# SwiGLU feed-forward on one core: full-array transposes at the start, a transposing load in two parts, and F tile 0 of the last token tiles in strips

## The chip, the cores and the metric

The kernel runs on one core of a Trainium2 chip. A core has a matrix engine (TensorE, "PE" in the profile, with its weight loads as "PEld"), VectorE ("DVE"), ScalarE ("ACT"), GpSimd ("POOL") and a queue engine that issues transfers (SyncE, "SP"). The metric is the device time of one execution in microseconds, as the median of several runs.

## The reference

```python
B, S, D, F = 1, 2048, 512, 1376       # x: (B, S, D); all inputs bfloat16

def reference(x, w_gate, w_up, w_down):
    g = silu(x @ w_gate)              # (S, F)
    u = x @ w_up                      # (S, F)
    return (g * u) @ w_down           # (S, D)
```

## The kernel before

The 2048 tokens are worked on in four chunks `c` of 512 (`SC`). D = 512 is four tiles of 128 (`KD`). F = 1376 is ten whole tiles of 128 (`NFF`) and a rest of 96. Gate and up products are computed with F on the partitions: for a chunk and an F tile there is a G group (gate) and a U group (up), each of four matmuls into one PSUM bank. ScalarE takes the silu of the G bank, VectorE multiplies it with the U bank and writes `hT_sb`. The rest of 96 is handled in X and Y groups, whose results stand in `hx_sb` and `hy_sb`. Groups take the eight PSUM banks in turn, and a bank is free when its reader eight groups earlier is done (`free`).

The order on each engine is written out by hand, and semaphores connect the engines: `s_P` counts finished groups of TensorE, `s_A` and `s_D` finished operations of ScalarE and VectorE, `s_X` finished transposes, `s_T` the turns told of below, and each load has one of its own.

The matmuls need x with D on the partitions (`xT_sb`). Tokens 0 to 255 come by two plain loads (`xn0` on SP, `xn1` on ACT) and are transposed on TensorE with an identity (L347). `RT` says in how many row pieces: the first 128 tokens go as two pieces of 64 rows, the second as one of 128. The transposes write PSUM, and for each 128 tokens VectorE (L292) and ScalarE (L281) copy two D tiles each into `xT_sb`. Ahead of that, TensorE multiplies constants (`warm`, L336): five matmuls of 512 columns and five of 128, and one of 128 (`N_COPY`) after the transposes. Tokens 256 to 511 come by one transposing load on SP (`x0b`, L93), which is queued behind the weight slabs of F tiles 0 to 3 and ahead of those of tiles 4 to 10. The three other chunks are transposing loads of 512 tokens each. All loads on SP but the first are issued in one stream without waits.

The first eight groups (F tiles 0 to 3, chunk 0) run in two passes: first over tokens 0 to 255, where the first group goes in two parts of 128 tokens, and then over tokens 256 to 511, which needs `x0b`. From then on every group takes 512 tokens at once.

The down product has tokens on the partitions of the output: 16 token tiles of 128, in four quads `q` of four tiles, one from each chunk. Its contraction has 43 pieces of 32 rows. In `strips` (L423), four matmuls of 32 rows run beside each other in four row groups of TensorE, each for another token tile of the quad and in another bank: this is a round. A call `strips(q, k, fks, ...)` is a phase: it makes one round for each F tile in `fks`, all with the row groups turned by `k`; the entry `NFF` is the rest of F. Ahead of the next phase of the same quad TensorE waits on `s_T` until the last round of the phase before is done (a turn). Quads 0 and 1 alternate phases. Quad 2 has phases of 10 or 11 rounds, and between two of them stands a phase of quad 3 with one round, the rest of F. What is left of quad 3 (F tiles 0 to 9) is then done with whole matmuls of 128 rows (L459), tile by tile; the last token tile is in two parts of 384 and 128 columns. Results are copied to `o_sb` by VectorE and ScalarE in turn, and SP stores them.

Of the kernel before, what the change touches and what calls it, by code (L numbers as in the profile page):

```python
# [8 lines left out]

N_WARM = 5  # L10
N_FILL = 5
N_COPY = 1


def bass_standalone__swiglu_ffn__prompt_kernel(nc, x, w_gate, w_up, w_down, out):
    _, S, D = x.shape
    F = w_gate.shape[1]
    P = 128
    KD = D // P
    NFF = F // P  # L20
    NFT = NFF + 1
    F_LAST = F - NFF * P
    SC = 512
    NSC = S // SC
    TPC = SC // P
    NST = S // P
    LASTA = 384
    HT = SC // 2
    NXN = HT // P
# [20 lines left out]
    with ExitStack() as es:  # L50
# [32 lines left out]
        def load_sem(name):  # L83
            loads[name] = sem(f"s_{name}")
            return loads[name]
# [6 lines left out]
        def load_x(eng, name, t0, t1):  # L92
            eng.dma_start_transpose(  # L93
                xT_sb[:, :, t0:t1], xf[t0:t1, :]
            ).then_inc(load_sem(name), 16)
# [10 lines left out]
        def load_gate(eng, a, b):  # L106
            load_w(eng, f"wg{a}", w_gate, 0, a * P, min(b * P, F))
# [4 lines left out]
        def load_xn(eng, i):  # L112
            eng.dma_start(xn_sb[:, i, :], xf[i * P:(i + 1) * P, :]).then_inc(load_sem(f"xn{i}"), 16)
# [5 lines left out]
        def loads_on_sync(sp):  # L119
            load_xn(sp, 0)  # L120
            load_gate(sp, *slabs[0])
            for a, b in slabs[1:3]:
                load_gate(sp, a, b)
                load_up(sp, a, b)
            load_x(sp, "x0b", HT, SC)
            for a, b in slabs[3:]:
                load_gate(sp, a, b)
                load_up(sp, a, b)
            load_w(sp, "wut", w_up, F - (F - 32), F - 32, F)
            for c in range(1, NSC):  # L130
                load_x(sp, f"x{c}", c * SC, (c + 1) * SC)
            sp.dma_start(
                wd_sb[:, 0:NFF, :], w_down[0:NFF * P, :].rearrange("(k p) d -> p k d", p=P)
            ).then_inc(load_sem("wd"), 16)
            load_sem("wdt")
            for y0 in (0, 64):
                sp.dma_start(wd_sb[y0:y0 + 64, T01, :], w_down[NFF * P:F - SR, :]).then_inc(loads["wdt"], 16)
            for x0 in range(0, P, SR):
                sp.dma_start(wd_sb[x0:x0 + SR, T2, :], w_down[F - SR:F, :]).then_inc(loads["wdt"], 16)
            sp.dma_start(wd_sb[0:F_LAST, TAIL, :], w_down[NFF * P:F, :]).then_inc(load_sem("wdl"), 16)  # L140
# [16 lines left out]
            g["readers"].append((eng, op["at"]))  # L157
            return op

        RT = [2, 1]  # L160
        T_BANK = [0, 2 * RT[0]]

        def tview(i, h):
            n, b0 = RT[i], T_BANK[i] + RT[i] * h
            return bank_all[:, b0:b0 + n, 0:P // n].bitcast(BF16).rearrange("p b (k t) -> p k b t", k=2)
# [47 lines left out]
        for i in range(NXN):  # L213
            for h, eng in enumerate("DA"):
                op = add_op(
                    eng, dict(readers=[]), kind="copy", ready=(s_X, 2 * sum(RT[:i]) + RT[i] * (h + 1)),
                    out=xT_sb[:, 2 * h:2 * h + 2, i * P:(i + 1) * P].rearrange("p k (b t) -> p k b t", b=RT[i]),
                    src=tview(i, h), stored=(None, 0),
# [13 lines left out]
        for at, t in enumerate(tiles):  # L232
            ob = at % NOS
            need = 16 * n_store[ob]
            halves = [(0, D)] if at < NST - 1 else [(0, LASTA), (LASTA, D)]
            for c0, c1 in halves:
                g = add_group("O", t=t, c0=c0, c1=c1)
                eng = "A" if at % 2 == 1 and c0 == 0 else "D"
                op = add_op(
                    eng, g, kind="copy", out=o_sb[ob][:, c0:c1], src=g["bank"][:, 0:c1 - c0],  # L240
# [54 lines left out]
        def on_tensor(pe):  # L295
            landed = set()

            def need(name, count=1):
                if name not in landed:
                    pe.wait_ge(loads[name], 16 * count)  # L300
                    landed.add(name)
# [13 lines left out]
            def gu_matmuls(g, n0, n1):  # L315
                c, ft = g["c"], g["ft"]
                if c > 0:
                    need(f"x{c}")
                if c == 0 and n1 > HT:
                    need("x0b")  # L320
                need(("wg" if g["kind"] == "G" else "wu") + str(slab_of[ft]))
                col = (0 if g["kind"] == "G" else UPH) + ft * P
                for dk in range(KD):
                    if c == 0 and dk % 2 == 0:
                        for i in range(n0 // P, min(n1 // P, NXN)):
                            after(*xt_ready[i, dk // 2])
                    ins = pe.matmul(  # L327
                        g["bank"][:, n0:n1], lhsT=w_sb[:, dk, col:col + P],
                        rhs=xT_sb[:, dk, c * SC + n0:c * SC + n1], start=(dk == 0), stop=(dk == KD - 1),
                    )  # L330
                if n1 == SC:
                    ins.then_inc(s_P, 1)

            def warm(n, width):
                for i in range(n):
                    pe.matmul(banks[NB - 1][:, 0:width], lhsT=ones_w, rhs=ones_m[:, 0:width], start=True, stop=True)  # L336
# [4 lines left out]
            for i in range(NXN):  # L341
                need(f"xn{i}")
                for dk in range(KD):
                    for b in range(RT[i]):
                        rt = P // RT[i]
                        r0 = rt * b
# [5 lines left out]
                        if dk % 2 == 1:  # L352
                            ins.then_inc(s_X, 1)

            warm(N_COPY, P)
            first = groups[0:NB]
            for n0, n1 in ((0, P), (P, HT)):
                gu_matmuls(first[0], n0, n1)
            for at in (1, 2, 3, 4, 6, 5, 7):
                gu_matmuls(first[at], 0, HT)  # L360
            for g in first:
                gu_matmuls(g, HT, SC)

            for g in groups[NB:NO]:
# [4 lines left out]
                elif kind == "X":  # L369
                    c = g["c"]  # L370
                    need(f"wg{slab_of[NFF]}")
                    need("wut")
                    for dk in range(KD):
# [3 lines left out]
                            start=(dk == 0), stop=(dk == KD - 1),  # L377
                        )
                    ins.then_inc(s_P, 1)
                elif kind == "Y":  # L380
                    need(f"wu{slab_of[NFF]}")
                    for dk in range(KD):
                        for c in (2 * g["pi"], 2 * g["pi"] + 1):
# [4 lines left out]
                                start=(dk == 0), stop=(dk == KD - 1),  # L388
# [8 lines left out]
                spare = (P + SR - 2 * Y_ROWS[c] - X_ROWS[c]) // SR  # L397
                return (spare + k) % TPC

            def strips(q, k, fks, start, stop):  # L400
                nonlocal n_turn
                quad = groups[NO + TPC * q:NO + TPC * (q + 1)]
                if start:
                    for g in quad:
                        free(g)
                else:
                    pe.wait_ge(s_T, turned[q])
                for fk in fks:
                    if fk == NFF:
                        need("wdt", 2 + TPC)  # L410
                    for c, g in zip(ORDER, quad):
                        t, c0, c1 = g["t"], g["c0"], g["c1"]
                        r0 = SR * strip_of(c, k)
                        tok = (t - c * TPC) * P
                        if fk < NFF:
                            h, w = hT_sb[r0:r0 + SR, fk, t * P:(t + 1) * P], fk
                        else:
                            after("D", t_ready[c])
                            if r0 == X_ROWS[c]:
                                h, w = hx_sb[r0:r0 + SR, c, tok:tok + P], T2  # L420
                            else:
                                h, w = hy_sb[r0:r0 + SR, c // 2, tok:tok + P], T01
                        ins = pe.matmul(  # L423
                            g["bank"][:, 0:c1 - c0], lhsT=h, rhs=wd_sb[r0:r0 + SR, w, c0:c1],
                            start=(start and fk == fks[0]), stop=(stop and fk == fks[-1]),
                            tile_position=(r0, 0), skip_group_check=True,
                        )
                        if stop and fk == fks[-1]:
                            ins.then_inc(s_P, 1)
                if not stop:  # L430
                    ins.then_inc(s_T, 1)
                    n_turn += 1
                    turned[q] = n_turn
# [4 lines left out]
            full, tailed = list(range(NFF)), list(range(NFT))  # L438
            for k in range(TPC):
                for q in (0, 1):  # L440
                    strips(q, k, full if k == 0 else tailed, k == 0, k == TPC - 1)
            for k in range(TPC):
                strips(2, k, full if k == 0 else tailed, k == 0, k == TPC - 1)
                if k < TPC - 1:
                    strips(3, k + 1, [NFF], k == 0, False)
            pe.wait_ge(s_T, turned[3])
            for g in groups[NO + TPC * (TPC - 1):]:
                t, c0, c1 = g["t"], g["c0"], g["c1"]
                last = g is groups[-1]
                if last:  # L450
                    free(g)
                    need("wdl")
                    pe.wait_ge(s_L, 1)
                for fk in (tailed if last else full):
                    if fk < NFF:
                        h, w = hT_sb[:, fk, t * P:(t + 1) * P], wd_sb[:, fk, c0:c1]
                    else:
                        h, w = hl_sb[0:F_LAST, :], wd_sb[0:F_LAST, TAIL, c0:c1]
                    ins = pe.matmul(  # L459
                        g["bank"][:, 0:c1 - c0], lhsT=h, rhs=w, start=(last and fk == 0),  # L460
                        stop=(fk == (NFF if last else NFF - 1)), skip_group_check=True,
                    )
                ins.then_inc(s_P, 1)
# [34 lines left out]
```

## Time and profile before

| what | value |
|---|---|
| median of 3 runs | 120.95 us (120.3 to 121.28) |
| the profiled execution | 120.11 us |
| its span in the profile | 118.8 us |
| TensorE busy | 115.5 us, 97% of the span, 982 matmuls |
| weight loads busy | 56.3 us, 47% |
| VectorE, ScalarE busy | 37.7 us and 35.0 us |
| strips (L423) in the chain that ended last | 28.71 us |
| whole matmuls of the last quad (L459) in it | 8.68 us |

The span is the time from the first to the last instruction of the program in the trace; the time of the execution has some 1.3 us around it. A row of the profile names the line of the kernel, the engine, the operation, what is written and read, how often, and then the busy time, the mean duration of one in ns and the idle time ahead of them with what ended it. Matmuls overlap, so the distance between the starts of two matmuls tells what one costs, and the duration of one is longer than that. A row of the chain or of the timeline begins with the start and the length in microseconds from the start of the span. The clock column of the profile shows 9 (full) in every slice; the half speed of the first four microseconds is seen only in the distances between matmuls.

### The profile page before, as it was taken

The numbers are of one execution on the slowest core, as the hardware profiler recorded it, in microseconds if no ns is written. First come the engines' busy times: TensorE is split into PE (matmuls) and PEld (weight loads), VectorE is DVE, ScalarE is ACT, GpSimd is POOL, SyncE is SP. The second block draws the span as 40 slices with busy tenths as digits, with TensorE's granted clock in tenths as the row PEclk, the third lists the DMA queues.
The fourth block names the chain that finished last, engine by engine and source line by source line (L and its number), as shares of the span: only waits on it lengthen the run. The fifth ranks groups of instructions, "written<-read, shape, count | busy, mean of one in ns | idle before, by whom it ended". The sixth has DMA issues, their size and how long they took to land.

```text
span 118.8 us, 2270 instructions
## 1 busy us (share of the span) xinstructions
PE 115.5 (97%) x982; PEld 56.3 (47%) x990; DVE 37.7 (32%) x57; ACT 35.0 (29%) x60; POOL 1.1 (1%) x7
## 2 busy tenths in 40 slices
PE   7999999999999999999999999999999999999993
PEld 2778444444444444444444444444444444444452
DVE  0106543344433444434444334460000044004220
ACT  4307334353244272343262442330000033003101
POOL 1000000000000000000000000010000000000000
PEclk9999999999999999999999999999999999999999
DMA  3999999960000000000000000000000027100512
GB/s 80 296 311 346 273 148 244 315 196 14 0 6 0 0 0 0 0 0 6 0 0 6 0 0 0 0 0 6 0 6 0 0 74 236 54 0 26 194 50 88
DMA packets 17610, 8.83 MB, mean 74 GB/s; under 512 B 10592, under 2 KB 17600, under 8 KB 17600
## 3 DMA queue, kind: packets, MB, share of 16 engines
q1 hardware_dynamic: 16928, 8.42, 27.3%
q10 hardware_dynamic: 672, 0.26, 0.9%
q8 instruction: 8, 0.13, 0.5%
q14 instruction: 2, 0.02, 0.0%
HBM read 4.75 MB, written 2.10 MB: 58 GB/s over the span
## 4 chain that ended last, share of the span: by engine, by line
PE 97%; issue 1%; DVE 0%
PE bank L327 58%; PE bank L423 24%; PE bank L459 7%; PE bank L374 3%; PE bank L336 2%; PE bank L385 2%; PE bank L347 1%; DVE o_sb L292 0%
## 5 line engine op out<-in xcount | busy, mean ns | idle before, releaser
L327 PE MATMUL bank<-xT_sb,w_sb 128*128 128x512 bf16 (+2 forms) x351 | 69.9, 357 | 0.3
L327 PEld LDWEIGHTS bank<-xT_sb,w_sb 128*128 128x128 bf16 x356 | 34.3, 98 | 35.0 <-DMA xT_sb<-in_x_dram 0.3
L288 DVE TENSOR_TENSOR hT_sb<-sg_sb,bank 128x512 bf16<-128x512 f32 x40 | 27.5, 687 | 40.6 <-PE bank L327 34.5
L281 ACT ACTIVATE sg_sb<-bank 128x512 f32<-128x512 f32 x40 | 23.8, 596 | 41.0 <-PE bank L327 40.9
L423 PE MATMUL bank<-wd_sb,hT_sb 32*128 32x512 bf16 x480 | 27.6, 374 | 0.0
L423 PEld LDWEIGHTS bank<-wd_sb,hT_sb 32*128 32x128 bf16 x480 | 12.0, 93 | 14.1 <-PE bank L423 1.1
L292 DVE CAST o_sb<-bank 128x512 bf16<-128x512 f32 (+1 forms) x9 | 5.5, 643 | 31.4 <-PE bank L423 25.3
L281 ACT ACTIVATE o_sb<-bank 128x512 bf16<-128x512 f32 (+1 forms) x8 | 4.3, 582 | 33.7 <-PE bank L423 27.2
L459 PE MATMUL bank<-wd_sb,hT_sb 128*128 128x512 bf16 (+2 forms) x49 | 8.6, 336 | 0.2 <-issue 0.2
L459 PEld LDWEIGHTS bank<-wd_sb,hT_sb 128*128 128x128 bf16 x50 | 4.5, 98 | 4.6 <-issue 0.4
L423 PE MATMUL bank<-wd_sb,hy_sb 32*128 32x512 bf16 (+1 forms) x32 | 4.2, 371 | 0.0
L374 PE MATMUL bank<-xT_sb,w_sb 128*128 128x512 bf16 x14 | 3.8, 379 | 0.1
L288 DVE TENSOR_TENSOR hx_sb<-sgx_sb,bank 32x512 bf16<-32x512 f32 x4 | 2.8, 691 | 3.5 <-ACT sgx_sb L281 3.5
L336 PE MATMUL bank<-const-bfloat16-1.0 128*128 128x128 bf16 (+1 forms) x11 | 3.0, 444 | 0.8 <-PEq L483 0.8
L281 ACT ACTIVATE sgx_sb<-bank 32x512 f32<-32x512 f32 x4 | 2.4, 588 | 4.5 <-PE bank L374 4.5
L423 PE MATMUL bank<-wd_sb,hx_sb 32*128 32x512 bf16 (+1 forms) x16 | 3.0, 371 | 0.0
L374 PEld LDWEIGHTS bank<-xT_sb,w_sb 128*128 128x128 bf16 x16 | 1.6, 98 | 1.9
L281 ACT ACTIVATE sgy_sb<-bank 64x512 f32<-64x512 f32 x4 | 2.4, 590 | 0.1
L336 PEld LDWEIGHTS bank<-const-bfloat16-1.0 128*128 128x128 bf16 x11 | 1.3, 135 | 2.2 <-issue 2.2
L385 PE MATMUL bank<-xT_sb,w_sb 128*64 128x512 bf16 x16 | 1.9, 382 | 0.0
L292 DVE COPY xT_sb<-bank 128x256 bf16<-128x256 bf16 x2 | 0.6, 292 | 4.1 <-PE bank L347 4.0
L270 ACT ACT_TABLE_LOAD x1 | 1.3, 1283 | 1.7 <-PEq L483 1.7
(17 smaller groups left out, 8.1 us busy)
## 6 DMA issues: line engine op xcount, KB each, us to landing
out_dram<-o_sb SPq DMA_DIRECT2D x15, 128.0 KB, 1.8
wd_sb<-in_w_down_dram SPq DMA_DIRECT2D x1, 1280.0 KB, 9.2
w_sb<-in_w_gate_dram SPq DMA_DIRECT2D x1, 480.0 KB, 5.6
w_sb<-in_w_up_dram SPq DMA_DIRECT2D x1, 448.0 KB, 6.3
w_sb<-in_w_gate_dram SPq DMA_DIRECT2D x1, 384.0 KB, 4.4
w_sb<-in_w_up_dram SPq DMA_DIRECT2D x1, 384.0 KB, 4.8
w_sb<-in_w_gate_dram SPq DMA_DIRECT2D x2, 128.0 KB, 3.1
w_sb<-in_w_gate_dram SPq DMA_DIRECT2D x1, 256.0 KB, 3.4
```

Of the source, the lines that this page charges most:

```text
L270: act.activation(adummy[:, 0:4], zero_c, ACT.Silu)
L281: act.activation(op["out"], op["src"], fn).then_inc(s_A, 1)
L288: ins = dve.tensor_tensor(op["out"], op["a"], op["b"], ALU.mult)
L292: ins = dve.tensor_copy(op["out"], op["src"])
L327: ins = pe.matmul(g["bank"][:, n0:n1], lhsT=w_sb[:, dk, col:col + P], rhs=xT_sb[:, dk, c * SC + n0:c * SC + n1], start=(dk == 0), stop=(dk ...
L336: pe.matmul(banks[NB - 1][:, 0:width], lhsT=ones_w, rhs=ones_m[:, 0:width], start=True, stop=True)
L347: ins = pe.matmul(tview(i, dk // 2)[:, dk % 2, b, :], lhsT=xn_sb[r0:r0 + rt, i, dk * P:(dk + 1) * P], rhs=ident[r0:r0 + rt, r0:r0 + rt], s ...
L374: ins = pe.matmul(g["bank"][:, :], lhsT=w_sb[:, dk, XC0:XC0 + P], rhs=xT_sb[:, dk, c * SC:(c + 1) * SC], start=(dk == 0), stop=(dk == KD - 1),
L385: ins = pe.matmul(g["bank"][y0:y1, :], lhsT=w_sb[:, dk, YC0:YC0 + 64], rhs=xT_sb[:, dk, c * SC:(c + 1) * SC], start=(dk == 0), stop=(dk == ...
L423: ins = pe.matmul(g["bank"][:, 0:c1 - c0], lhsT=h, rhs=wd_sb[r0:r0 + SR, w, c0:c1], start=(start and fk == fks[0]), stop=(stop and fk == f ...
L459: ins = pe.matmul(g["bank"][:, 0:c1 - c0], lhsT=h, rhs=w, start=(last and fk == 0), stop=(fk == (NFF if last else NFF - 1)), skip_group_ch ...
```

## The change

Three places change.

- Start: both blocks of 128 tokens are transposed in whole pieces of 128 rows (`RT = [1, 1]`), which takes eight transposes in place of twelve, and their banks move to 0 to 3. The constant matmul behind the transposes is gone.
- Tokens 256 to 511: `x0b` becomes two transposing loads of 128 tokens, `x0b` and `x0c`. In the second pass the first group runs in two parts of 128 tokens, and only the second needs `x0c`.
- Down product: quad 3 takes F tile 0 in strips as well. Its phase between the phases of quad 2 has now two rounds (F tile 0 and the rest of F) in place of one. The fourth row turn of F tile 0 is a round of its own in the middle of the last phase of quad 2, which is cut in two halves; the second half has no wait for a turn. The whole matmuls of quad 3 begin with F tile 1, except in the last part of 128 columns, which keeps all its matmuls.

```diff
-N_COPY = 1
...
-            load_x(sp, "x0b", HT, SC)
+            load_x(sp, "x0b", HT, HT + P)
+            load_x(sp, "x0c", HT + P, SC)
...
-        RT = [2, 1]
-        T_BANK = [0, 2 * RT[0]]
+        RT = [1] * NXN
+        T_BANK = [2 * i for i in range(NXN)]
...
                 if c == 0 and n1 > HT:
                     need("x0b")
+                if c == 0 and n1 > HT + P:
+                    need("x0c")
...
-            warm(N_COPY, P)
             first = groups[0:NB]
             for n0, n1 in ((0, P), (P, HT)):
                 gu_matmuls(first[0], n0, n1)
             for at in (1, 2, 3, 4, 6, 5, 7):
                 gu_matmuls(first[at], 0, HT)
-            for g in first:
+            for n0, n1 in ((HT, HT + P), (HT + P, SC)):
+                gu_matmuls(first[0], n0, n1)
+            for g in first[1:]:
                 gu_matmuls(g, HT, SC)
...
-            def strips(q, k, fks, start, stop):
+            def strips(q, k, fks, start, stop, turn=True):
...
-                else:
+                elif turn:
                     pe.wait_ge(s_T, turned[q])
...
-            for k in range(TPC):
-                strips(2, k, full if k == 0 else tailed, k == 0, k == TPC - 1)
-                if k < TPC - 1:
-                    strips(3, k + 1, [NFF], k == 0, False)
+            for k in range(TPC - 1):
+                strips(2, k, full if k == 0 else tailed, k == 0, False)
+                strips(3, k + 1, [0, NFF], k == 0, False)
+            half = NFT // 2
+            strips(2, TPC - 1, tailed[:half], False, False)
+            strips(3, 0, [0], False, False)
+            strips(2, TPC - 1, tailed[half:], False, True, turn=False)
             pe.wait_ge(s_T, turned[3])
...
-                for fk in (tailed if last else full):
+                for fk in (tailed if last else full[1:]):
```

## The prediction

> **What bounds the kernel now.** I read the profile in this order: the busy shares and the chain that ended last, then the waits, then the instruction timeline at the places that the change touches, and the DMA issues last. Busy shares and chain first, by line, with the pieces of the chain in order of time:
>
> ```profile
> PE 115.5 (97%) x982; PEld 56.3 (47%) x990; DVE 37.7 (32%) x57; ACT 35.0 (29%) x60; POOL 1.1 (1%) x7
> ...
> PE 97%; issue 1%; DVE 0%
> ```
>
> ```profile
> 3.67 0.77 PE bank L347 x12
> 4.44 0.06 PE bank L336
> 4.49 3.76 PE bank L327 x36
> 8.26 0.02 issue
> 8.27 3.67 PE bank L327 x32
> ...
> 79.40 28.71 PE bank L423 x522
> 108.11 0.16 issue
> 108.27 8.68 PE bank L459 x50
> 116.95 0.02 issue
> 116.97 0.29 DVE o_sb L292
> ```
>
> TensorE is the bound from end to end. Where TensorE streams, one matmul of 512 columns starts 0.216 us after the other, one of 384 after 0.163, one of 256 after 0.109 and one of 128 after 0.056. A round of four 32-row strips starts 0.216 after the other too, as if the four were one. So the change can only act through the number of TensorE slots and through the holes between them. The waits and the timeline show three kinds of hole near the change:
>
> ```profile
> PEld bank L423 <- PE bank L423: 1.1, 3, 0.3
> ...
> PEld bank L327 <- DMA xT_sb<-in_x_dram: 0.3, 1, 0.3
> ```
>
> ```profile
> 4.06 0.80 ACT L281 ACTIVATE xT_sb<-bank 128x256 bf16<-128x256 bf16 x2 [0.83 <-PE bank L347]
> ```
>
> ```profile
> 3.92 1.47 SPq L93 DMA_TRANSPOSE xT_sb<-in_x_dram  x1
> 5.43 0.57 SPq L98 DMA_DIRECT2D w_sb<-in_w_gate_dram  x1
> 6.06 0.50 SPq L98 DMA_DIRECT2D w_sb<-in_w_up_dram  x1
> ```
>
> First, the three waits L423 on itself: the wait at each turn of the third group, where one round stands between two phases. The phases begin at 100.31, 102.93 and 105.56, so 12 rounds take 2.627 instead of 12 x 0.2158 = 2.590: a turn costs 0.037 (the 0.3 in the row is idle time of the weight loads, most of it hidden under the running round). Second, the first pass over tokens 0-255 ends at 8.09 (last start 7.982 + 0.109), and the second starts at 8.272, when the load of tokens 256-511 has landed (8.23): a hole of 0.18. Third, the copies after the transposes, told below.
>
> **Transposes in the full array.** Removed: eight 64-row transposes (starts 3.615 to 3.775, 0.025 apart), a hole of 0.17 before the first full one at 3.945, and one filler at 4.274. Added: four more transposes of 128 rows. Until about 4.2 a 128-wide matmul starts 0.107 after the one before, afterwards 0.056, so TensorE runs at half speed here. I place the eight new ones at 3.615, 3.70, 3.81, 3.91, 4.02, 4.13, 4.22 and 4.27 (first step 0.083 as between the full ones now, then 0.107, then the faster ones). A copy starts about 0.04 after the end of its transpose, which lasts 0.297 at half speed and 0.219 at full speed. The copies of 0.292 (DVE) and 0.384 (ACT) then move so: first DVE copy from 3.954 to 4.04, first ACT copy from 4.059 to 4.25, second DVE copy from 4.363 to 4.41. The second ACT copy waits for the first: it ends at 4.25 + 0.384 + 0.031 + 0.384 = 5.05, instead of 4.858. The last pair of matmuls of the first G group waits for it (4.913 now), and everything behind it in TensorE's order with it: first pass **+0.19**. Lower bound: 0, if TensorE is at full speed by then (steps of 0.056 put the fourth start at 3.78, where the eighth 64-row one stands now). Upper bound 0.22, with a first step of 0.107. The filler costs nothing now: the first weight slab lands at 4.30, after it has started, and the first real matmul at 4.391 is behind that.
>
> The row here is the hole of 0.17 between the 64-row and the 128-row transposes. The Trainium skill, TensorEngine Tiling (Array Packing), Key Properties, says that a change of tiling mode drains TensorE; the trace agrees with that hole, and by it alone this part would gain 0.17. The timeline says that the gain is given back, since the ACT copies and not TensorE set the last start.
>
> **Two transposing loads.** The 0.18 hole hides most of the 0.19: the first pass now ends at 8.09 + 0.19 = 8.28, and the first half of the load is there well before. In the packets of the trace the load's data moves from 6.35 to 7.5, behind the slabs ahead of it, and the semaphore follows 0.7 later; half the data gives 6.95 + 0.7 = 7.65. The second half is due at 8.28 + 4 x 0.056 = 8.50, and lands at 8.23 if issuing keeps ahead. A 256-token issue costs 1.467, a 512-token one at least 2.245 (the last of the three), so a 128-token one lies between 0.73 (half) and 1.47 (the same); from these two rows an estimate is 1.08. Two end at 3.918 + 2 x 1.08 + 0.05 = 6.13, ahead of the data's turn at 6.95. At 1.47 each they end at 6.90. All later SP issues move by 0 to 1.5: the gate slab of tiles 4-6 lands at 9.83 and is used at 11.78, its up slab at 10.89 for 12.64, x1 at 17.09 for 23.2, w_down at 28 for 79. Nothing there is late even by the upper bound. Start of the second pass: 8.28 against 8.272, **+0.01**. Its first group takes 8 x 0.056 instead of 4 x 0.109: **+0.01**.
>
> **F tile 0 in strips.** Removed from the last phase: three matmuls of 512 and one of 384, 3 x 0.216 + 0.163 = 0.810. Added: four rounds of strips, 4 x 0.216 = 0.863, since a round takes its widest strip. Net **+0.05**. Each of the three turns now has two rounds in it, 0.43 instead of 0.216, where 0.037 was missing: **-0.11** (bounds 0, if the wait isn't one for the last strip's end, and -0.11). The round put between the halves of the last phase of group three waits for a turn five rounds back, 1.08 earlier, and the half behind it has no wait at all. The hole at the change from strips to the full array (0.534 from start to start, 0.318 too long) stays. The last tiles now take nine slots, 1.94, and an eviction 0.60 to 0.69, so stores keep their place behind the end.
>
> **Sum.** +0.01 +0.01 +0.05 -0.11 = **-0.04**, against the profiled execution's 120.11 (span 118.8 and 1.3 around it): 120.07. The median of the runs shown is 120.95, 0.84 above the profiled one, and the runs spread over 1 us. The rows suggest one cause for that spread, full speed reached later than 4.2: there the 0.18 hole is already covered before the change, and the transposes cost their part. With half speed throughout, the last ACT copy ends at 4.96 now and 5.06 after: +0.10 instead of +0.02, the sum is +0.04. On the median that is 120.91 to 120.99; I take **120.95**, no change. A difference of about 1% (1.2 us) is what a measurement of this kernel can tell from none.
>
> **Rivals.** (1) Slower: full speed is reached later. The removed filler and the eight short transposes leave less plain matmul work between 3.5 and 4.9, and holes of about 0.1 to 0.2 before each pair that waits for a copy. If TensorE stays at half speed for one more stretch as long as the first (0.84 to 4.18, 3.34 us), it loses 1.67, less the 0.18 that the hole covers: +1.5, 122.4. It decides once the delay passes 0.36 (two times 0.18); beyond 2.8 it is over 1%. For it: the transposes now fill exactly the time in which the speed changes. Against it: the ten fillers up to 3.46, most of that stretch, are untouched. The Trainium skill, TensorE: Matmul & The Clock Gate, Part 4, says that transposes don't count as busy time for the clock in the way that matmuls do, and Part 1 gives a free-running window of about 3.4 us; no run here shows either, though the 3.34 is close to it.
>
> (2) Slower: each 128-token load costs what a 256-token load costs, issue and lag. The second lands at 6.90 + 2.85 (8.23 less the issue's end at 5.385) = 9.75, 1.25 after 8.50: 122.2. Against it: of the 2.85, almost 1 is waiting behind other data.
>
> (3) Faster but within 1%: TensorE is at full speed at the transposes, the first pass doesn't move, the second starts at 8.09: -0.18 +0.01 -0.06 = -0.23, 120.7.
>
> (4) The turns stay as they are, because something other than the distance makes them: +0.07, 121.0.
>
> (5) Faster by over 1%: the start becomes regular, so that the median falls to the profiled run's and (3) comes on top: -0.84 - 0.23, 119.9. Only the spread speaks for it.
>
> **How the numbers follow.** Forecast 0.54, (3) 0.14, (4) 0.06: together 0.74 within 1%. (1) 0.12 and (2) 0.05: 0.17 slower. (5) and the like 0.09 faster. The likeliest case alone, with the spread of the runs, is 120.3 to 121.4; reaching toward (5) below and half way to (1) above gives 120.1 to 121.7.
>
> **What would show it.** Turns: the three waits of L423 on itself are gone or under 0.01 of path, and the strips (now L426) take 136 rounds of 0.216, 29.4 to 29.5. Last phase (L459, now L462): 7.87. Start: first pass ends near 8.28 with the last ACT copy at 5.05, no DMA wait at the second pass, its first half landed near 7.65 and its second near 8.25. The forecast is wrong if 128-wide matmuls still start 0.107 apart after 4.6, if a DMA wait appears at tokens 384-511, or if any later slab waits.

## The result, and the profile after

The changed kernel takes 120.44 us in the median of 20 runs (120.22 to 120.89), the kernel before 120.85 (120.22 to 121.28). The ratio is 0.9972, with a 95% interval of 0.9959 to 0.9985: 0.34 us faster, between 0.18 and 0.50. This is within 1%, but it is not the "no change" that was forecast.

The profiled execution of the changed kernel took 120.27 us, a little more than that of the kernel before (120.11, one of the fastest of all its runs). So the two pages, laid side by side, show a loss at the start and a gain at the end. The pieces of the chain of the changed kernel, in order of time:

```profile
2.82 3.92 DMA w_sb<-in_w_gate_dram
6.74 0.05 issue
6.78 5.42 PE bank L329 x52
...
79.67 29.41 PE bank L426 x540
109.08 0.16 issue
109.24 7.87 PE bank L465 x46
117.11 0.02 issue
117.13 0.29 DVE o_sb L292
```

The strips begin at 79.67 instead of 79.40 (+0.27). From there the end is reached sooner: 29.41 + 0.16 + 7.87 = 37.44 instead of 28.71 + 0.16 + 8.68 = 37.55 (-0.11). The start hangs on a weight slab in this execution: the chain runs through the load of the gate slab of F tiles 2 and 3. The waits of the weight loads say the same, and two rows of before are missing, the waits of the strips for themselves and the wait for x:

```profile
PEld bank L329 <- DMA w_sb<-in_w_gate_dram: 0.4, 1, 0.4
...
PEld bank L329 <- DMA w_sb<-in_w_up_dram: 0.2, 1, 0.2
```

The SP queue's timeline (start, length, instruction) shows the two transposing issues merged into one row, 2.85 where one took 1.47; singly they take 1.54 and 1.26:

```profile
3.93 2.85 SPq L92 DMA_TRANSPOSE xT_sb<-in_x_dram  x2
6.82 0.58 SPq L97 DMA_DIRECT2D w_sb<-in_w_gate_dram  x1
```

ScalarE's timeline, the two copies after the transposes:

```profile
4.25 0.66 ACT L281 ACTIVATE xT_sb<-bank 128x256 bf16<-128x256 bf16 x2 [1.01 <-PE bank L349]
```

They begin at 4.25, as forecast, but both are done 0.66 later, although one lasts 0.38. The second begins 0.28 after the first (4.53), while the first still runs.

One execution can't explain a median here. The start differs from execution to execution by more than the change moves, and the experiments had to find what is common to many.

### The profile page after: what moved, and what is told of

It is laid out like the page before. It is cut to its first block, busy times and chain, and to the rows that moved or that the text cites. A ratio compares the mean times of both kernels' runs of the same rounds, so it can differ in the third digit from the quotient of the medians.

```text
span 119.0 us, 2293 instructions
## 1 busy us (share of the span) xinstructions
PE 115.6 (97%) x993; PEld 59.6 (50%) x1001; DVE 37.7 (32%) x57; ACT 34.8 (29%) x60; POOL 1.1 (1%) x7
## 4 chain that ended last, share of the span: by engine, by line
PE 92%; DMA 3%; SPq 2%; issue 1%; DVE 0%
PE bank L329 57%; PE bank L426 25%; PE bank L465 7%; DMA w_sb<-in_w_gate_dram 3%; PE bank L377 3%; PE bank L388 2%; SPq L97 1%; SPq L112 0%; DVE o_sb L292 0%
## 5 line engine op out<-in xcount | busy, mean ns | idle before, releaser
L426 PE MATMUL bank<-wd_sb,hT_sb 32*128 32x512 bf16 x496 | 29.0, 374 | 0.0
L426 PEld LDWEIGHTS bank<-wd_sb,hT_sb 32*128 32x128 bf16 x496 | 15.3, 93 | 11.5 <-issue 0.4
L465 PE MATMUL bank<-wd_sb,hT_sb 128*128 128x512 bf16 (+2 forms) x45 | 7.8, 333 | 0.2 <-issue 0.2
L426 PE MATMUL bank<-wd_sb,hy_sb 32*128 32x512 bf16 (+1 forms) x32 | 5.0, 371 | 0.0
L338 PE MATMUL bank<-const-bfloat16-1.0 128*128 128x512 bf16 (+1 forms) x10 | 2.8, 466 | 0.8 <-PEq L489 0.8
L426 PEld LDWEIGHTS bank<-wd_sb,hy_sb 32*128 32x128 bf16 x32 | 1.6, 93 | 0.6
```

The costliest lines, as they stand in the source:

```text
L426: ins = pe.matmul(g["bank"][:, 0:c1 - c0], lhsT=h, rhs=wd_sb[r0:r0 + SR, w, c0:c1], start=(start and fk == fks[0]), stop=(stop and fk == f ...
L465: ins = pe.matmul(g["bank"][:, 0:c1 - c0], lhsT=h, rhs=w, start=(last and fk == 0), stop=(fk == (NFF if last else NFF - 1)), skip_group_ch ...
```

## The experiments

Theory A: the start is a race between TensorE and the loads; in most executions the first pass ends before tokens 256-511 have landed, and the split takes that wait away, while the transposes cost next to nothing. Its rivals: the gain is at the end alone (B), the transposes bring it (D), or it arises from when TensorE comes to full speed (E, G).

### One part at a time

E1 is the split alone (the two `load_x` lines, the wait for `x0c`, and the first group in parts). E2 is the strips alone. E3 is the transposes alone (`RT`, `T_BANK`, and `warm(N_COPY, P)` left out). E4 is the changed kernel without the split.

> The kernel before with the transposing load of tokens 256-511 in two parts and nothing else. Theory A (in most executions the wait for that load is longer than the 0.18 us of the profiled one, and the split hides the four matmuls of the first half, 4 x 0.056): about 0.2 us faster, ratio 0.998. Theory B (the split gains nothing, since the second half lands no earlier, and the whole gain of the change is elsewhere): ratio 1.000. In the trace: A wants the first half to land before the second by more than 0.2 us.

Measured: 120.75, ratio 0.9989 (0.9968 to 1.0010), which fits both theories. In its trace the second half lands 0.42 after the first, and TensorE waits for neither.

> The kernel before with F tile 0 of the last quad in strips and nothing else. By the two traces (strips start to last eviction 37.64 us before, 37.53 after): 0.11 us faster, ratio 0.999; strips 29.41 us and whole matmuls 7.87 in the chain. The theory of the prediction, in which a round costs its widest strip, wants 0.06 us and 29.46. The start is that of the kernel before: one more sample of when tokens 256-511 land (8.23 us in its one trace; theory A of the split wants mostly later).

Measured: 120.56, ratio 0.9982 (0.9956 to 1.0009). The chain:

```profile
79.81 29.41 PE bank L423 x540
109.22 8.03 PE bank L462 x47
117.24 0.02 issue
117.27 0.29 DVE o_sb L292
```

The 0.16 of issue is inside the 8.03 here; the sum is 37.44 again. From the start of the first strip to the end of the last eviction it is 37.82, against 37.93 in the kernel before. E4, `after` and all others with this part have 37.82 as well, and E1 and E3, without it, have 37.93. This 0.11 is the same in every trace.

> The kernel before with eight transposes of 128 rows and no constant matmul behind them, and nothing else. Theory A (the wait for tokens 256-511 covers it): ratio 1.000. Theory C (first pass later by the 0.05 to 0.19 us that the copies come later, and this shows): 0.05 to 0.19 us slower, ratio 1.0005 to 1.0015. Theory D (the transposes are what brings the gain): faster by 0.2 us.

Measured: 120.64, ratio 0.9996 (0.9975 to 1.0018). The wait for tokens 256-511 is in the trace:

```profile
PEld bank L326 <- DMA xT_sb<-in_x_dram: 0.3, 1, 0.3
...
PEld bank L326 <- DMA w_sb<-in_w_gate_dram: 0.2, 1, 0.2
```

> The changed kernel with tokens 256-511 in one transposing load again. Theory A: the gain of the strips alone remains, 0.11 us, ratio 0.999, and the trace waits for that load ahead of the second pass. Theory B (the split is worth nothing): the same ratio as the whole change, 0.997.

Measured: 120.62, ratio 0.9985 (0.9963 to 1.0007), with a wait of 0.05 for the load.

The times of the single parts can't tell 0.1 from 0: every interval includes both. The traces can, but each is one execution.

### The strips: how a round of unequal strips costs

E6 takes two F tiles of the last quad in strips in place of one:

```diff
-                strips(3, k + 1, [0, NFF], k == 0, False)
+                strips(3, k + 1, [0, 1, NFF], k == 0, False)
...
-            strips(3, 0, [0], False, False)
+            strips(3, 0, [0, 1], False, False)
...
-                for fk in (tailed if last else full[1:]):
+                for fk in (tailed if last else full[2:]):
```

> The changed kernel with F tiles 0 and 1 of the last quad in strips (eight rounds in place of four). Theory F (the four row groups run on by themselves, so the strip of 384 columns shortens its row group, by 0.054 us a tile): strips start to last eviction as in the changed kernel, 37.53 us, since 0.863 - 0.054 replaces 0.810. Theory of the prediction (a round costs its widest strip): 37.58.

Measured: 120.56, ratio 0.9972 (0.9957 to 0.9986). The chain:

```profile
79.98 30.22 PE bank L426 x556
110.20 0.16 issue
110.36 7.06 PE bank L465 x42
117.42 0.02 issue
117.44 0.29 DVE o_sb L292
```

30.22 + 0.16 + 7.06 = 37.44, as in the changed kernel (first strip to last eviction 37.82 in both). Four more rounds cost 0.81 and not 0.86, exactly what they replace: theory F holds. The timeline of the changed kernel shows how, at the first phase of quad 3:

```profile
100.50 0.32 PE L426 MATMUL bank<-wd_sb,hy_sb 32*128 32x384 bf16 x1
100.55 0.37 PE L426 MATMUL bank<-wd_sb,hx_sb 32*128 32x512 bf16 x1
...
100.66 2.43 PE L426 MATMUL bank<-wd_sb,hT_sb 32*128 32x512 bf16 x40
102.82 0.37 PE L426 MATMUL bank<-wd_sb,hy_sb 32*128 32x512 bf16 x1
102.92 0.37 PE L426 MATMUL bank<-wd_sb,hx_sb 32*128 32x512 bf16 x1
```

The phase has two rounds, each with one strip of 384 columns in the same row group. After the first, that row group starts at 100.50, 0.05 ahead of the other three, although its strip is the last of its round in the program. After the second it runs 0.10 ahead (100.66), and is still 0.10 ahead ten rounds later (102.82 against 102.92). Quad 3 goes through all four row groups, so each of them is shortened by one such strip per F tile, 0.054. The Trainium skill, TensorEngine Tiling (Array Packing), Key Properties, says that tiles operate independently and can run their matmuls in parallel; the trace agrees, down to that 0.10.

### The start: order of the loads

E5 queues the two loads of tokens 256-511 ahead of the slab of F tiles 2 and 3; E7 is the same with one load.

```diff
-            for a, b in slabs[1:3]:
+            for a, b in slabs[1:2]:
...
-            for a, b in slabs[3:]:
+            for a, b in slabs[2:]:
...
-            first = groups[0:NB]
+            first = groups[0:NB // 2]
...
-            for at in (1, 2, 3, 4, 6, 5, 7):
+            for at in (1, 2, 3):
...
-            for g in groups[NB:NO]:
+            for g in groups[NB // 2:NO]:
```

> The changed kernel with the two loads of tokens 256-511 queued ahead of the slab of F tiles 2 and 3, and only the first four groups in two passes (the other four take 512 tokens at once). Theory A (the start is a race between TensorE and the order in which loads land): the first four groups need x at about 6.9 us, the slab about 1.7 later, so every wait of the start goes, and the kernel is 0.1 to 0.3 us faster than the changed one, ratio to the kernel before 0.995 to 0.997. Theory E (the start is set by when TensorE reaches full speed, not by loads): the same ratio as the changed kernel.

Measured: 120.85, ratio 0.9992 (0.9976 to 1.0008). No weight load waits for x in its trace, and yet it is no faster than the changed kernel: beside it, the changed kernel (`after_again`, below) had a mean 0.19 lower, with an error of 0.10. In this execution TensorE came to full speed only at 6.5 us, so one trace doesn't show what an early one does. Theory A's number is refuted.

> As e5 with tokens 256-511 in one load. Theory A: the first four groups wait for it by up to 0.2 us if it lands after 6.9, else no wait; ratio 0.996 to 0.998. If e7 equals e5, the split is worth nothing once the order is right.

Measured: 120.72, ratio 0.9982 (0.9961 to 1.0004), no different from E5 within the intervals. Its trace waits 0.25 for the load, a little more than expected, and also for the slab that now stands behind it:

```profile
PEld bank L326 <- DMA xT_sb<-in_x_dram: 0.4, 1, 0.4
...
PEld bank L326 <- DMA w_sb<-in_w_gate_dram: 0.2, 1, 0.2
```

The gate slab of F tiles 2 and 3 lands at 8.62 here and at 8.78 in E5, over 1 us later than in the kernels with the old order (6.25 to 7.33). So the order can move the wait from x to the slab. TensorE loses only 0.08 by that in E7 and nothing in E5; whether it loses more in executions with an early full speed, and whether that is what the order costs, no trace shows.

### Held and cold starts

Two ways to take the varying start out. In the held kernels all loads wait for eleven dummy operations of ScalarE and are issued from 8.03 on; in the four traces TensorE is at full speed by 4.5 to 7.0. `N_HOLD` is 19, `N_LATE` 11, `N_WARM` 12 and `N_FILL` 2 there. In the cold ones the constant matmuls ahead of the transposes are left out.

```diff
+            sp.wait_ge(s_W, 1)
             loads_on_sync(sp)
...
+            act.activation(adummy[:, 0:4], zero_c, ACT.Silu)
+            for i in range(N_LATE):
+                ins = act.activation(late_sb[:, i, :], ones_m, ACT.Copy)
+            ins.then_inc(s_W, 1)
+            act.wait_ge(s_W, 1)
             loads_on_scalar(act)
-            act.activation(adummy[:, 0:4], zero_c, ACT.Silu)
...
+            warm(N_HOLD, SC)
+            pe.wait_ge(s_W, 1)
             warm(N_WARM, SC)
```

> The kernel before with its start held back: all loads wait for eleven dummy activations on ScalarE (some 7 us), and TensorE multiplies constants until then and for as long again as the first load takes, so that it is at full speed in every execution before the first transpose. It computes the same; about 7 us slower than the kernel before. It is the base for the other three. Theory A (at full speed the start follows the loads): the trace shows a wait of 0.18 us or more for tokens 256-511, and the spread of the runs is smaller than the 1.3 us of the kernel before.

> The changed kernel with the same hold. Against the held kernel before: theory A, 0.24 to 0.36 us faster (0.11 at the end, the rest the wait for tokens 256-511); theory G (the gain arises in executions that reach full speed late, where TensorE and not the loads set the start), 0.11.

> The kernel before with the load in two parts, and the hold. Against the held kernel before: theory A, 0.18 to 0.28 us faster; theory G, 0.

> The kernel before with eight transposes of 128 rows and no constant matmul behind them, and the hold. Against the held kernel before: 0 where the wait for tokens 256-511 covers it. First G matmul of 256 columns after the landing of the first 128 tokens: 1.55 us in the kernel before, 1.60 in the changed one (both at full speed from 4.2 us on); the copies should now be the same or later by up to 0.05.

Measured: 127.90, 127.68, 127.63 and 127.67, from 5 or 6 runs each that spread over 0.6 to 0.9. The differences of the means from h_before (0.14, 0.18 and 0.11) are not clear of their errors of 0.16 to 0.19. The traces are of use: the wait for tokens 256-511 is 0.11 in h_before and 0.13 in h_transposes, less than the 0.18 that theory A wanted, and nothing in h_after and h_split. From the first transpose to the first G matmul of 256 columns it is 1.22 with the 64-row transposes (h_split) and 1.26 with the 128-row ones (h_transposes, and also the changed kernel in `after_again` and `after_third`): the transposes cost 0.03 at full speed. In h_before and h_after (1.32 and 1.54) a late weight slab falls into this stretch. The smaller spread that theory A wanted isn't there: the standard deviations are 0.25 to 0.33, and 0.30 in the kernel before, run beside them. So, as far as so few runs tell, the time varies as much when TensorE is at full speed from the first transpose on.

> The kernel before without the ten constant matmuls ahead of the transposes, so that TensorE reaches full speed later and is behind the loads in every execution. Base for c_after; 0.3 to 1.5 us slower than the kernel before, and no wait for tokens 256-511 in the trace.

> The changed kernel without the ten constant matmuls. Against c_before, theory A: 0.11 us faster, which is the end alone. If it is 0.3 us faster all the same, the split isn't what gains at the start.

Measured (9 and 12 runs): 121.64 and 121.48, ratios to the kernel before 1.0074 (1.0044 to 1.0105) and 1.0056 (1.0033 to 1.0079). The means differ by 0.27, with an error of 0.21, so the times can't tell the 0.11 of theory A from 0.3. The trace of c_before waits 0.08 for tokens 256-511, against what was expected, that of c_after not at all. At half speed the same distance, first transpose to first matmul of 256 columns, is 1.69 in c_before and 1.675 in c_after, so the transposes cost nothing there, although the last copy ends 0.07 later (1.43 after the first transpose, against 1.36).

### The split when the load is late

```diff
+            load_gate(sp, *slabs[3])
             load_x(sp, "x0b", HT, SC)
-            for a, b in slabs[3:]:
+            load_up(sp, *slabs[3])
+            for a, b in slabs[4:]:
```

> The kernel before with the load of tokens 256-511 queued behind the gate slab of F tiles 4 to 6 (384 KB), so that it lands over 1 us later. Base for late_split: the trace shows one wait of 0.8 to 1.6 us ahead of the second pass, ratio 1.006 to 1.012.

> The same with the load in two parts and the first group in two parts. Theory A: the first half lands 0.4 to 0.5 us ahead of the second, but TensorE has only four matmuls of 0.056 for it and then waits for the second, so the split takes 0.2 to 0.3 us off, however long the wait. Rival: the second half lands later than the one load did, since a 128-token issue costs nearly as much as a 256-token one (1.54 and 1.26 against 1.47 to 2.46), and the gain is below 0.1.

Measured: 121.95 (4 runs) and 121.44 (6 runs), ratios 1.0096 (1.0067 to 1.0126) and 1.0067 (1.0042 to 1.0092). The waits of the weight loads, first of late_one, then of late_split:

```profile
PEld bank L329 <- DMA xT_sb<-in_x_dram: 1.3, 1, 1.3
```

```profile
PEld bank L332 <- DMA xT_sb<-in_x_dram: 0.7, 2, 0.5
```

One long wait becomes two shorter ones. Counted from the landing of the slab ahead of the load, the one load lands after 1.01, the halves after 0.54 and 0.99. TensorE has four matmuls of 0.056 for the first half and then waits for the second. The second group of the second pass begins 1.50 after that slab in late_one and 1.27 in late_split: the split takes 0.23 off a wait of 1.2. The rival, under 0.1, is refuted. The means of the times differ by 0.40, with an error of 0.14, which agrees with 0.23 but doesn't fix it.

### The changed kernel again, with and without the split

> The changed kernel once more, unchanged: a second sample of its start and of its ratio. By the traces so far: last phase and strips gain 0.11 us, the transposes cost 0 to 0.05, the split takes away a wait of 0 to 0.18: ratio 0.9975 to 0.999. If the ratio is below 0.997, the start gains more than the waits that the traces of the unsplit load show (0.18, 0, 0.19 and 0.05 us), and something else is at work.

Measured: 120.66, ratio 0.9977 (0.9958 to 0.9995).

> The changed kernel a third time. By the traces, 0.11 us at the end and 0 to 0.19 at the start: ratio 0.9975 to 0.999.

Measured: 120.58, ratio 0.9982 (0.9967 to 0.9997).

> The changed kernel with tokens 256-511 in one load, a second time. Theory A: 0.1 us slower than the changed kernel, ratio to the kernel before 0.999, and the trace waits for that load or misses it by less than 0.1.

Measured: 120.80, ratio 0.9989 (0.9970 to 1.0007). Its waits:

```profile
PEld bank L326 <- DMA w_sb<-in_w_gate_dram: 0.8, 2, 0.4
...
PEld bank L326 <- DMA xT_sb<-in_x_dram: 0.3, 1, 0.3
```

All runs together, as means with the standard error: the kernel before 120.81 (146 runs, 0.02), the changed kernel 120.53 (44 runs, 0.04), the changed kernel without the split 120.67 (24 runs, 0.06). So the split is worth 0.14, with an error of 0.07, and the rest of the change the same. (Each against the kernel before run beside it, the changed kernel gains 0.30, with an error of 0.05, and the one without the split 0.14, with 0.07.) Two errors are no more than a hint; what shows the split's part is the trace. The starts of the traces, by instruction:

| kernels | wait of TensorE for tokens 256-511, us |
|---|---|
| one load: before, E2, E3, E4, h_before, h_transposes, c_before, no_split_again | 0.18, 0, 0.19, 0.05, 0.11, 0.13, 0.08, 0.19 |
| two loads: the changed kernel three times, E1, E6, h_after, h_split, c_after | 0 in all eight |

The mean of the first row is 0.12, and no wait in it is longer than 0.19: that most executions wait longer than the 0.18 of the first profile, as theory A had it ahead of E1, is refuted. The loads themselves set this limit. Where tokens 256-511 come in one load (before, E2, E3, E4, c_before, no_split_again), it lands 1.92 to 1.98 after the gate slab of F tiles 2 and 3, and the rest of the first pass takes TensorE 1.75 from its first matmul on that slab. In E3 and no_split_again TensorE starts on the slab as soon as it lands, and waits 0.19; in E4, c_before and E2 it starts 0.20 to 0.28 after the landing, and waits 0.05, 0.08 and 0.

With the 0.11 of the end this makes 0.23, inside the 0.18 to 0.50 of the first comparison. The pooled means give 0.28 with an error of 0.04; whether 0.05 more are hidden in the start stays open.

## Why the prediction was wrong, point by point

**What bounds the kernel** was right: TensorE from end to end, and every part of the gain is a hole or a slot on it.

**Transposes** was the step that failed most: "The second ACT copy waits for the first" and so +0.19. In the changed kernel it began 0.28 after the first, not 0.41, and was done at 4.91 instead of 5.05. The first matmul of 256 columns came at 5.086 instead of 5.035, that is +0.05. The experiments give 0.03 at full speed and nothing at half speed, where +0.10 was reckoned. The 0.031 that the sum put between the copies was misread: in the profile before, the last transpose ends at 4.437 and the second copy begins 0.037 later, the usual step, so that copy waited for its transposes, and no row at the copies showed how closely one can follow another. A row that does stood in the same profile, on the evictions of this very engine:

```profile
95.77 1.08 ACT L281 ACTIVATE o_sb<-bank 128x512 bf16<-128x512 f32 x2 [16.98 <-PE bank L423]
```

Two of 0.59 to 0.60 done in 1.08: the second starts 0.49 after the first. A chain of operations on one engine is to be priced by the distance of starts, not by durations.

**Two transposing loads**: the hole was seen, and its size (0.18) was near the upper end of what the other traces show (0 to 0.19). But the sum let it be filled by the 0.19 that didn't exist. With the measured 0.05 the first pass ends at 8.14, and the start of the second pass becomes 8.14 - 8.272 = -0.13 in place of +0.01. The landings were nearly as forecast: 8.23 and 8.63 in a trace whose slab ahead landed 0.47 later than before. Counted from that slab, the one load lands after 1.16 to 1.20 (before, E2 to E4) and the halves after 0.70 and 1.10 to 1.17 (forecast: 7.65 and 8.25 after 7.06, that is 0.6 and 1.2). The issue of 128 tokens was estimated at 1.08, with 1.47 as the upper bound, and took 1.54 and 1.26 (the first of the two 2.04 in E1); as argued, nothing behind it was late. Rival (2), a late second half, is refuted by this.

**Strips**: +0.05 for the four rounds was mis-sized, since "a round takes its widest strip" is false: measured 0.00 (E6). The turns were right: -0.11, and their three waits are gone. Together -0.11 instead of -0.06. The whole sum, with what was measured, is -0.13 + 0.01 - 0.11 = -0.23, and not -0.04. The prediction also took 1% as the least that can be told from none; 20 runs of each kernel told 0.3%.

**The reading of the spread** failed too. The distance of the matmuls does show full speed reached at different times: in after_third and after_again it is there when TensorE begins the transposes, at 3.73 and 3.85, behind a pause from about 3.5 on; in E4 it comes only at 6.7, with the other kernels that begin like the one before in between. The Trainium skill, TensorE: Matmul & The Clock Gate, Part 1, has a free-running window of about 3.4 us; a range of about 3 agrees with it. But I concluded that in the typical run, with full speed reached late, the hole is covered. The traces with late full speed mostly still wait: E3 (full speed from 5.5) 0.19, E4 (6.7) 0.05, c_before (6.9) 0.08, and only E2 (5.7) doesn't. And late full speed isn't what the time follows most closely. The loads vary too, and the time goes with them:

| trace | full speed from, us | gate slab of F tiles 2 and 3 lands, us | time of that execution, us |
|---|---|---|---|
| after_third | 3.7 or sooner | 6.41 | 119.99 |
| E2 | 5.7 | 6.66 | 120.41 |
| after_again | 3.85 or sooner | 6.86 | 120.40 |
| E4 | 6.7 | 7.16 | 120.90 |
| no_split_again | 4.6 | 7.25 | 120.98 |

Over the ten traces with the constant matmuls and the old order of loads (before, E1 to E4, E6, no_split_again and the changed kernel three times) the correlation of the time with the landing of this slab is 0.94, and with the start of full speed 0.68. Together with the held kernels, which spread as much at full speed, this points to the loads; what moves the landing stays open.

**Rivals.** What came is rival (3) by its size: -0.23 forecast, the wait gone and the end gained. That its sum meets the -0.23 above is luck: it had the first pass unmoved, which moved by 0.05, and the strips at -0.06, which were -0.11. Its condition, full speed at the transposes, isn't needed; the overlap of the copies does it. Rival (1), a later full speed, didn't show: kernels with the 128-row transposes reached it between about 3.5 and 6.7, those with the 64-row ones between 4.2 and 6.6. Rival (4) is refuted by the missing waits, rival (5) by the median. The time lies inside the range.

## What to carry to other kernels

Price a chain of operations on one engine by the distance between their starts in the trace, and look for that distance on the same engine even in another stage. Strips of unequal width in several row groups don't wait for each other, so they cost the longest row group over the whole phase and not the widest strip of each round. Splitting a load helps by the work that can be done on its first part, here four matmuls of 0.056, and where starts vary by 1 us, count the waits in many traces rather than compare two, and look at what the time goes with from trace to trace before naming a cause of the spread.

## What was not expected of the hardware

ScalarE starts the next copy of 0.38 only 0.28 after the one before, and no sooner: in after_again the transposes of the second were done at 4.46, and it began at 4.55, 0.28 after the first, and not the usual 0.04 after its transposes. Row groups of TensorE stay out of step, here by 0.10, over a phase of ten rounds. A transposing load of 128 tokens occupies the issuing queue for 1.26 to 2.04 us (2.04 in E1), nearly as long as one of 256 (1.47 in the kernel before to 2.60 in c_before).
